# Separate PSUM banks for the last output pieces, an earlier release of the last down bank, and new landing times for the opening, in a one-core attention and SwiGLU kernel

## The chip, the cores and the metric

The kernel runs on one core of a Trainium2 chip. Times are device microseconds (us) of that core. The engines are TensorE (PE, whose weight loads are shown as PEld), VectorE (DVE), ScalarE (ACT), GpSimd (POOL) and SyncE (SP), which issues most of the DMAs. The metric is the median time of the kernel's runs.

## The reference

The input x has 2048 tokens of 512 values. It is normalised per token, xn. One branch is sliding-window attention with 32 heads of 16 and a window of 256 keys, followed by a projection with wo. The other is a SwiGLU network of width 1792 whose result goes through another silu and gates the attention's output.

```python
x = A_x
xn = _layernorm(x, axis=-1)
s = _A_ref(xn, A_wqkv, A_wo)                # window attention, then @ wo
g = _silu(_B_ref(xn, B_w_gate, B_w_up, B_w_down))
return x + s * g                             # _B_ref: (silu(x@w_gate) * (x@w_up)) @ w_down
```

Everything is float32. The kernel splits the operands of each large product into a high and a low float32r part and adds three products: high by high, high by low and low by high (`PAIRS`).

## The kernel before

**How PE is used.** A product over 128 rows of weights is cut into two halves of 64 rows, half 0 and half 1 (`half(r)`), which lie in the upper and lower half of the PE array and stream side by side. For each output item half 0 makes its matmuls first, into a PSUM bank; then DVE copies one column of the bank (`handover`, L582 to L584, tile `ho`), and half 1 may add its matmuls to the same bank. So half 1 trails half 0 by about one item. `LAG` keeps it at least seven 512-column matmuls behind while half 0 has work.

**The items.** The 2048 tokens are four chunks of 512. Work units come in an order made by `dense_order`: `Proj` (tile a, queries and keys), `Values` (vp), `GateUp` (g and u), `Down` (d, in four quarters q of the hidden width) and `Wo` (s, the output projection). Each unit has two items. An item of `Moving` units (vp, d, s) holds two pieces of 128 tokens, n = 0 and 1, side by side in one bank: columns 0 to 255 and 256 to 511. `act` gives the stationary operand (tokens), `w` the moving one (weights). Attention (tiles b, mt, c, pv) is woven into the dense items through the list `extra`.

**What sets the order.** A planner runs at build time. It keeps a clock for each PE half and a queue for DVE (V), ACT (S), POOL (G) and the DMA queue of SP (D), with a cost for each operation that `do` is given, a ready time and a slack; `pump` issues what is ready. Nothing of this runs on the chip: the result is one fixed order of instructions on each engine, and on the chip each engine waits for semaphores in that order. A change of a ready time or a cost moves instructions throughout the program.

**The opening.** `load_first` loads the first 512 tokens as four tiles `xt` and three pieces of the value weights `wr`, some over ACT's DMA queue, some over SP's. DVE takes mean and variance (L339 to L344); ACT subtracts the mean (`center`, L347); PE transposes (`x_turn`, L443, tiles xp); ACT and DVE make the high and the low part of the transposed tokens (xh in L465, xl in L462). Meanwhile ACT copies the high part of each weight piece (`high`, wh, L392) and POOL subtracts for the low part (`low`, wl, L396). The first items on PE are vp. `lands`, `lanes`, `stream_at` and the last argument of `split` are the times at which the planner takes the first loads to land. `warm_up` fills PE with matmuls of no use to the result (tile warm).

**The last down quarter.** For q = 3 `done` of `Down` makes three steps: `one` (DVE, L893) adds the sum so far in `gp` (SBUF) to the bank, in place; `two` (ACT, L897) takes tanh of the bank into `dt`; `three` (DVE, L900) reads `dt` and the bank and writes `gp`. The bank is free after `three`.

**The end.** The last unit is `Wo` of chunk 3, column half 1, items s3_1_0 and s3_1_1. For the second item the products of half 0 with k = 2 and 3 are taken out of half 1 and done in a separate group, `rest` (L587, planned by `rest_pairs`), whose two pieces share one bank. When a piece of an item is complete, `last_part` makes `mul` (L1077: half of gp by the bank into `yl`), then `add` (L1083 on DVE for the second item, which adds `yr`; L1085 on POOL for the first) and stores it; `yr` is made from `rest` by L1047 and L1052. The last store is issued by ACT, the others by SP.

Of the kernel before, what the change touches and what calls it, by code (L numbers as in the profile page):

```python
# [60 lines left out]
def tile_window_attention_swiglu_gate(  # L61
# [258 lines left out]
    def load_first():  # L320
# [8 lines left out]
        lands = (3.8, 4.75, 6.4, 7.3)  # L329
# [57 lines left out]
        def split(raw, j, r, t):  # L387
# [18 lines left out]
            for a in (0, 512):  # L406
# [6 lines left out]
                do("S", t, 0.53, lambda a=a: high(a), done, 0.3 + 0.001 * a)  # L413
# [13 lines left out]
        free_at["D"] = 6.8  # L427
        free_at["S"] = 4.7
        stream_at[0] = 5.7
        lanes[:] = [5.4, 6.3, 6.4, 7.2, 7.3, 7.8, 8.2, 9.2]  # L430
        for i in range(4):
            do("V", lands[i], 1.05 if i != 1 else 1.45, lambda i=i: stats(i), lambda t, i=i: after_stats(t, i), -1.0)
        split(wr[0], 0, 0, 5.5)
        split(wr[1], 1, 1, 8.3)
        split(wr[1], 1, 0, 9.3)

    def x_turn(i):
# [10 lines left out]
        if i == 0:  # L448
            warm_up(warm, 1)
# [341 lines left out]
    class Values(Moving):  # L791
# [12 lines left out]
        def mms(self, i, r, pb):  # L804
# [4 lines left out]
            order = [(t, k, 0, b) for t in range(2) for k in ((0, 1), (2, 3)) for b in range(2)]  # L809
# [11 lines left out]
        def gate(self, i, r, m):  # L821
            if self.c:
                return 0.0
            kp, a, b = (m // 4 % 2, 0, m // 2 % 2) if m < 16 else ((m - 16) // 4, 1, 0)
# [32 lines left out]
    class Down(Moving):  # L857
# [19 lines left out]
        def done(self, i, pb, t, free):  # L877
# [14 lines left out]
            def one():  # L892
                nc.vector.tensor_tensor(p2, g, p2, op=ALU.add)  # L893

            def two():
                tiles.append(take(f"dt{c}_{hf}_{i}", (P, 2, 256)))
                nc.scalar.activation(tiles[0], p2, AF.Tanh, scale=0.5)  # L897

            def three():
                nc.vector.scalar_tensor_tensor(g, tiles[0], 1.0, p2, op0=ALU.add, op1=ALU.mult)  # L900
                give(tiles[0])

            def after_one(t):
                do("S", t, 0.5, two, lambda t: do("V", t, 0.61, three, after_three, PRIO - 0.5), PRIO - 0.5, room(1))

            def after_three(t):
                free(t)
# [7 lines left out]
    class Wo(Moving):  # L915
# [15 lines left out]
        def mms(self, i, r, pb):  # L931
            if r == 0 or (self.c, self.hf) != (NCH - 1, 1):
                yield from super().mms(i, r, pb)
                return
            w = [t.rearrange("p (k n) -> p k n", n=256) for t in self.wts(1)]
            nk = KC - 2 * i
            for t in range(2):
                tok = slice((2 * i + t) * P, (2 * i + t + 1) * P)
                for k in range(nk):
                    for a, b in PAIRS:  # L940
                        def go(first, last, t=t, k=k, a=a, b=b, tok=tok):
                            mm(
                                pb[:, t * 256 : t * 256 + 256], self.act(k, a)[half(1), tok],
                                w[b][half(1), k, :], first, last,
                            )
                            if (t, k, a) == (0, nk - 1, 1):
                                last_part(i, 0, pb, now[0] + 0.35)
# [796 lines left out]
```

## Time and profile before

| | |
|---|---|
| median of 3 runs | 853.81 us (853.38 to 854.67) |
| profiled execution | 852.52 us |
| its span, from the first to the last recorded instruction or landing | 850.6 us |
| outside the span | 1.92 us |
| PE busy | 843.2 us, 99% of the span |
| DVE, ACT, POOL busy | 502.7, 489.2, 630.0 us |
| granted clock of PE | 0.999 |

The profiled execution is 1.29 us below the median of the runs. In the rows, a line number is that of the kernel before (the changed kernel's lines are 2 lower between L448 and the class `Wo`, and the same from there to L1600), L587 is the helper `mm` through which all dense matmuls go, so its rows are told apart by their tiles, and a row of the timeline gives start, duration, engine, line, operation, written and read tiles, shapes and, in brackets, the idle time ahead of it with what ended it.

### The profile page before, as it was taken

To read this page: it belongs to the slowest core of one execution; us is meant where nothing else is said; L and a number is where in the kernel's file an instruction comes from. 1 tells how busy PE (TensorE), PEld (TensorE's weight loads), DVE (VectorE), ACT (ScalarE), POOL (GpSimd) and SP (SyncE) were. 2 spreads that over 40 slices of the span, in tenths; PEclk is the share of its full clock that TensorE was granted. 3 is DMA by queue.
4 is the path that set the end of the run, shared out by engine and by line. 5 is a ranking of instruction groups with operands and counts; after the bars stand their busy time and mean duration, and the time that the engine had idled before them with its cause. 6 is when DMAs were issued, how large, how long until landed. Compare 5 with 4: busy or idle time off the path is not lost.

```text
span 850.6 us, 29962 instructions
## 1 busy us (share of the span) xinstructions
PE 843.2 (99%) x11948; PEld 793.0 (93%) x11948; DVE 502.7 (59%) x1676; ACT 489.2 (58%) x969; POOL 630.0 (74%) x908
## 2 busy tenths in 40 slices
PE   8999999999999999999999999999999999999997
PEld 8999999899999999989999999998999999999897
DVE  4266576656756675655656876565655666653335
ACT  7526664546666557564666657655556665655521
POOL 6639675769777687678777997667689777787861
PEclk9999999999999999999999999999999999999999
DMA  8486847665876995666776977665766688735251
GB/s 205 123 200 141 224 121 208 161 158 114 196 161 195 231 225 125 139 174 167 173 179 166 221 176 193 135 169 132 199 162 169 137 197 187 195 103 138 80 152 53
DMA packets 70098, 140.00 MB, mean 165 GB/s; under 512 B 14710, under 2 KB 23670, under 8 KB 69960
## 3 DMA queue, kind: packets, MB, share of 16 engines
q1 hardware_dynamic: 69496, 137.44, 66.4%
q8 instruction: 94, 1.54, 0.8%
q10 hardware_dynamic: 464, 0.66, 0.3%
q14 instruction: 44, 0.36, 0.2%
HBM read 107.87 MB, written 29.62 MB: 162 GB/s over the span
## 4 chain that ended last, share of the span: by engine, by line
PE 98%; DMA 1%; DVE 0%; SPq 0%; issue 0%; DVEq 0%
PE u L587 20%; PE g L587 19%; PE d L587 19%; PE a L587 10%; PE pv L1414 8%; PE c L1377 6%; PE s L587 6%; PE vp L587 5%; PE b L1229 5%; DMA xt<-x 1%; PE xp L607 0%; PE xp L443 0%; DVE yl L1077 0%; PE mt L1263 0%; PE rest L587 0%; DVE st L339 0%
## 5 line engine op out<-in xcount | busy, mean ns | idle before, releaser
L552 POOL TENSOR_TENSOR wl<-wr,wh 128x512 fp32r<-128x512 f32 (+1 forms) x258 | 305.2, 1197 | 85.4 <-ACT wh L548 58.5
L1237 DVE CUSTOM_DVE_ANT_0 jk<-b,maskb 128x384 bf16<-128x384 f32 (+2 forms) x512 | 271.3, 530 | 103.7 <-PE b L1229 63.1
L587 PE MATMUL d<-wh,hh 64*128 64x256 f32 x1792 | 266.8, 279 | 0.0
L1337 ACT ACTIVATE p<-c 128x512 f32<-128x512 f32 (+2 forms) x384 | 198.0, 571 | 93.2 <-PE c L1377 89.6
L587 PEld LDWEIGHTS d<-wh,hh 64*128 64x128 f32 x1792 | 227.9, 185 | 1.2 <-issue 0.6
L587 PE MATMUL d<-wl,hh 64*128 64x256 f32 x896 | 204.6, 278 | 0.0
L587 PE MATMUL g<-xh,wl 64*128 64x512 f32 x448 | 158.7, 395 | 0.0
L587 PE MATMUL u<-xh,wl 64*128 64x512 f32 x448 | 157.6, 393 | 0.0
L587 PE MATMUL g<-xh,wh 64*128 64x512 f32 x448 | 157.5, 392 | 0.0
L587 PE MATMUL u<-xh,wh 64*128 64x512 f32 x448 | 157.3, 393 | 0.0
L587 PE MATMUL g<-xl,wh 64*128 64x512 f32 x448 | 157.1, 392 | 0.0
L587 PE MATMUL u<-xl,wh 64*128 64x512 f32 x448 | 157.1, 393 | 0.0
L548 ACT ACTIVATE wh<-wr 128x512 fp32r<-128x512 f32 (+1 forms) x258 | 142.8, 589 | 11.1 <-DMA wr<-wgu 3.0
L587 PEld LDWEIGHTS d<-wl,hh 64*128 64x128 f32 x896 | 145.1, 185 | 0.3
L1349 POOL TENSOR_SCALAR_AFFINE_SELECT p<-p 128x256 f32<-128x256 f32 x256 | 102.0, 411 | 38.0 <-ACT p L1337 37.2
L1229 PE MATMUL b<-k,q 48*128 48x384 f32 (+2 forms) x512 | 110.6, 328 | 0.0
L742 POOL TENSOR_TENSOR hh<-h,hh 128x512 fp32r<-128x512 f32 x56 | 72.6, 1297 | 50.3 <-ACT hh L738 49.2
L1353 POOL TENSOR_SCALAR_AFFINE_SELECT p<-p 128x256 f32<-128x256 f32 x224 | 91.6, 411 | 20.2 <-ACT p L1337 18.6
L587 PE MATMUL a<-xl,wh 64*128 64x512 f32 x256 | 96.7, 390 | 0.0
L587 PE MATMUL a<-xh,wl 64*128 64x512 f32 x256 | 96.4, 391 | 0.0
L587 PE MATMUL a<-xh,wh 64*128 64x512 f32 x256 | 96.3, 392 | 0.0
L1377 PE MATMUL c<-q,k 49*128 49x128 f32 (+2 forms) x704 | 95.4, 298 | 0.0
(121 smaller groups left out, 2108.4 us busy)
## 6 DMA issues: line engine op xcount, KB each, us to landing
wr<-wgu SPq DMA_DIRECT2D x112, 256.0 KB
k<-qkd SPq DMA_DIRECT2D x48, 192.0 KB
wr<-wqk SPq DMA_DIRECT2D x32, 256.0 KB
qkd<-qkh SPq DMA_DIRECT2D x32, 256.0 KB
qkd<-qkl SPq DMA_DIRECT2D x32, 256.0 KB
q<-qkd SPq DMA_DIRECT2D x64, 128.0 KB
wr<-wdn SPq DMA_DIRECT2D x32, 256.0 KB
od<-ev SPq DMA_DIRECT2D x32, 256.0 KB
```

What stands on the lines that cost most here:

```text
L548: nc.scalar.activation(wtile[j][0][pr, a:b], raw[pr, a:b], AF.Copy)
L552: nc.gpsimd.tensor_tensor(lo[pr, a:b], raw[pr, a:b], f32(hi[pr, a:b]), op=ALU.subtract)
L587: return nc.tensor.matmul(pb, a, b, start=first, stop=last, skip_group_check=True)
L742: nc.gpsimd.tensor_tensor(hl[:, 1, :], self.h, f32(hl[:, 0, :]), op=ALU.subtract)
L1229: nc.tensor.matmul(pb[:, :n], qs[u % 3][r : r + 48, p, qb * P : (qb + 1) * P], ks[u % 3][r : r + 48, p, lo : lo + n], start=True, stop=True,)
L1237: nc.vector.tensor_tensor_reduce(junk[:, :n], pb[:, :n], maskb[:, 3 * P - n :], 1.0, -3.0e38, ALU.add, ALU.max, m[:, col : col + 1],)
L1337: nc.scalar.activation(t[:, h, :], pc[:, :n], AF.Exp, scale=DH ** -0.5)
L1349: nc.gpsimd.affine_select(s, s, [[0, 2], [1, P]], ALU.is_ge, 0.0, base=0, channel_multiplier=-1)
L1353: nc.gpsimd.affine_select(s, s, [[0, 2], [-1, P]], ALU.is_gt, 0.0, base=0, channel_multiplier=1)
L1377: nc.tensor.matmul(pc[:, at0 : at0 + w], ks[u % 3][r : r + 49, p, k0 : k0 + P], qs[u % 3][r : r + 49, p, qb * P : qb * P + w], start=(i == ...
L1414: nc.tensor.matmul(pbs[r][0][32 * j : 32 * j + 32, q0:q1], vt[half(r), (4 * c + kb) % VT, VW * (4 * g + j) : VW * (4 * g + j) + 32], t[hal ...
```

## The change

It has four parts.

1. **Banks of the last items.** For s3_1_0 and s3_1_1 the second piece of 128 tokens gets a bank of its own, `second[i]` (s2_0 and s2_1), from the pool that attention uses; `rest` gets two banks, rest0 and rest1. `last_part` and `rest_pairs` read the banks given. The planner adds a `handover` copy for each second bank.
2. **Last down quarter.** `one` writes its sum into `gp` instead of the bank, and the bank is free after it; `two` and `three` read `gp`. `three` is planned at 0.8 instead of 0.61 and with a slack of 0.0 instead of -1.0.
3. **Opening times.** `lands`, `lanes`, `stream_at`, `free_at["D"]` and the times of `split` get other values, the latter one for each 512-column piece. One `warm_up` matmul behind the first transposes is left out.
4. **Order in the first vp items.** All products of one pair of k for both token pieces come ahead of the next pair of k, instead of one token piece after the other; `gate` follows.

```diff
-        lands = (3.8, 4.75, 6.4, 7.3)
+        lands = (4.4, 5.5, 7.8, 8.7)
...
-        split(wr[1], 1, 0, 9.3)
+        split(wr[1], 1, 0, (11.9, 11.9))
...
-        if i == 0:
-            warm_up(warm, 1)
...
-            order = [(t, k, 0, b) for t in range(2) for k in ((0, 1), (2, 3)) for b in range(2)]
+            order = [(t, k, 0, b) for k in ((0, 1), (2, 3)) for b in range(2) for t in range(2)]
...
             def one():
-                nc.vector.tensor_tensor(p2, g, p2, op=ALU.add)
+                nc.vector.tensor_tensor(g, g, p2, op=ALU.add)
...
-                nc.scalar.activation(tiles[0], p2, AF.Tanh, scale=0.5)
+                nc.scalar.activation(tiles[0], g, AF.Tanh, scale=0.5)
...
-                nc.vector.scalar_tensor_tensor(g, tiles[0], 1.0, p2, op0=ALU.add, op1=ALU.mult)
+                nc.vector.scalar_tensor_tensor(g, tiles[0], 1.0, g, op0=ALU.add, op1=ALU.mult)
...
             def after_one(t):
-                do("S", t, 0.5, two, lambda t: do("V", t, 0.61, three, after_three, PRIO - 0.5), PRIO - 0.5, room(1))
+                free(t)
+                do("S", t, 0.5, two, lambda t: do("V", t, 0.8, three, after_three, 0.0), PRIO, room(1))
...
+                po = (pb, self.second[i])[t][:, :256]
...
+                        mm(po, self.act(k, a)[half(r), tok], w[b][half(r), k, :], r == 0 and n == 0, r == 1 and end)
+                        if r and end and t == 0:
+                            last_part(i, 0, po, now[0] + 0.35)
...
+                self.second[i] = bank(rb_free, f"s2_{i}")[0]
...
-        pb, tag = bank(rb_free, "rest")
+        pbs = [bank(rb_free, f"rest{n}")[0][:, :256] for n in range(2)]
...
-                y, gp[:, 2 * i + n, 256:512], 0.5, pb[:, 256 * n : 256 * n + 256], op0=ALU.mult, op1=ALU.mult
+                y, gp[:, 2 * i + n, 256:512], 0.5, pb, op0=ALU.mult, op1=ALU.mult
...
+            if isinstance(u, Wo) and (u.c, u.hf) == (NCH - 1, 1):
+                do("V", t, 0.1, lambda: handover(u.second[i]), None, -1.0)
```

Two places show how the rows move. The first is the end of PE's program, where half 0 is in `rest` and half 1 passes from the first to the second token piece of s3_1_0. Before, both pieces of each stand in one bank:

```order
L587 MATMUL s3_1_0_17156<-wl120_17023,xh0_79 128x256
L587 MATMUL rest_17264<-wl120_17023,ox0_16958 128x256
L587 MATMUL s3_1_0_17156<-wh120_17022,xl0_80 128x256
L587 MATMUL rest_17264<-wh120_17022,ox1_16959 128x256
L587 MATMUL s3_1_0_17156<-wh120_17022,xh0_79 128x256
L587 MATMUL rest_17264<-wh120_17022,ox0_16958 128x256
```

Now the same place has a bank for each piece (s2_0 is the second piece of s3_1_0):

```order
L585 MATMUL rest0_17261<-wh120_17124,ox1_16971 128x256
L585 MATMUL s3_1_0_17145<-wl120_17125,xh0_79 128x256
L585 MATMUL rest1_17262<-wh120_17124,ox0_16970 128x256
L585 MATMUL s3_1_0_17145<-wh120_17124,xl0_80 128x256
L585 MATMUL rest1_17262<-wl120_17125,ox0_16970 128x256
L585 MATMUL s2_0_17146<-wh120_17124,xh0_79 128x256
```

The matmuls are the same in number; what they write to is not, and `rest` stands a few matmuls further ahead of half 1.

At the same end DVE's last rows before work on the two pieces of the last item together:

```order
L1047 SCALAR_TENSOR_TENSOR yr1_17297<-gp_83,rest_17264 128x256
L1077 SCALAR_TENSOR_TENSOR yl0_1_17301<-gp_83,s3_1_0_17156 128x256
L1052 TENSOR_TENSOR yr1_17297<-yr1_17297,xr3_1_1_17078 128x256
L1077 SCALAR_TENSOR_TENSOR yl1_0_17311<-gp_83,s3_1_1_17210 128x256
L1077 SCALAR_TENSOR_TENSOR yl1_1_17321<-gp_83,s3_1_1_17210 128x256
L1083 TENSOR_TENSOR yl1_0_17311<-yl1_0_17311,yr0_17282 128x256
L1083 TENSOR_TENSOR yl1_1_17321<-yl1_1_17321,yr1_17297 128x256
```

Now the first piece is finished ahead of the second:

```order
L1047 SCALAR_TENSOR_TENSOR yr1_17296<-gp_83,rest1_17262 128x256
L1077 SCALAR_TENSOR_TENSOR yl0_1_17308<-gp_83,s2_0_17146 128x256
L1052 TENSOR_TENSOR yr1_17296<-yr1_17296,xr3_1_1_17058 128x256
L1077 SCALAR_TENSOR_TENSOR yl1_0_17318<-gp_83,s3_1_1_17204 128x256
L1083 TENSOR_TENSOR yl1_0_17318<-yl1_0_17318,yr0_17280 128x256
L1077 SCALAR_TENSOR_TENSOR yl1_1_17328<-gp_83,s2_1_17205 128x256
L1083 TENSOR_TENSOR yl1_1_17328<-yl1_1_17328,yr1_17296 128x256
```

The first piece's add (L1083) has moved between the two products (L1077).

The second place is the opening on PE, from the first vp matmul to the transposes of the fourth token tile. Before:

```order
L587 MATMUL vp0_0_0_183<-wh0_151,xh1_81 128x256 x2
L587 MATMUL vp0_0_0_183<-wl0_152,xh1_81 128x256 x2
L443 MATMUL xp0_2_191<-ident_68,xt0_2_103 128x128 x2
L443 MATMUL xp0_3_192<-ident_68,xt0_2_103 128x128 x2
L587 MATMUL vp0_0_0_183<-wh0_151,xh1_81 128x256 x2
L587 MATMUL vp0_0_0_183<-wl0_152,xh1_81 128x256 x2
L587 MATMUL vp0_0_0_183<-wh0_151,xh1_81 128x256 x2
L443 MATMUL xp0_2_191<-ident_68,xt0_3_106 128x128 x2
L443 MATMUL xp0_3_192<-ident_68,xt0_3_106 128x128 x2
```

Now:

```order
L585 MATMUL vp0_0_0_178<-wh0_157,xh1_81 128x256 x4
L585 MATMUL vp0_0_0_178<-wl0_158,xh1_81 128x256 x4
L585 MATMUL vp0_0_0_178<-wh0_157,xh1_81 128x256 x3
L443 MATMUL xp0_2_201<-ident_68,xt0_2_103 128x128 x2
L443 MATMUL xp0_3_202<-ident_68,xt0_2_103 128x128 x2
L585 MATMUL vp0_0_0_178<-wh0_157,xh1_81 128x256
L585 MATMUL vp0_0_0_178<-wl0_158,xh1_81 128x256 x4
L443 MATMUL xp0_2_201<-ident_68,xt0_3_106 128x128 x2
L443 MATMUL xp0_3_202<-ident_68,xt0_3_106 128x128 x2
```

The transposes of the third token tile (xt0_2) have moved behind eleven vp matmuls instead of four, those of the fourth (xt0_3) behind sixteen instead of ten.

On ACT the same stretch reads before:

```order
L465 ACTIVATE xh1_81<-xp0_0_154 128x2x256
L347 ACTIVATE xt0_2_103<-xt0_2_103,nm0_90 128x512
L465 ACTIVATE xh1_81<-xp0_1_155 128x2x256
L347 ACTIVATE xt0_3_106<-xt0_3_106,nm0_90 128x512
L392 ACTIVATE wh1_211<-wr1_100 64x512 x3
```

and now:

```order
L463 ACTIVATE xh1_81<-xp0_0_151 128x2x256
L463 ACTIVATE xh1_81<-xp0_1_152 128x2x256
L347 ACTIVATE xt0_2_103<-xt0_2_103,nm0_90 128x512
L392 ACTIVATE wh1_197<-wr1_100 64x512
L347 ACTIVATE xt0_3_106<-xt0_3_106,nm0_90 128x512
L392 ACTIVATE wh1_197<-wr1_100 64x512
```

The second xh copy has moved ahead of the centering of the third tile, and a piece of wh1 between the centerings of the third and the fourth.

More of the change, by code (lines that the diff above doesn't have):

```diff
@@ L976, in done @@
             if (c, hf) == (NCH - 1, 1):
-                last_part(i, 1, pb, t)
+                last_part(i, 1, self.second[i][:, :256], t)
                 return
@@ L1035, in rest_ready @@
             return None
-        return latest([rest["t"], wready.get(len(weighted)), bank_time(rb_free)])
+        return latest([rest["t"], wready.get(len(weighted)), bank_time(rb_free, 2)])
     def rest_pairs():
-        pb, tag = bank(rb_free, "rest")
+        pbs = [bank(rb_free, f"rest{n}")[0][:, :256] for n in range(2)]
         w = [t.rearrange("p (k n) -> p k n", n=256) for t in wtile[len(weighted)]]
@@ L1047, in mul @@
                 nc.vector.scalar_tensor_tensor(
-                    yr, gp[:, 2 + n, 256:512], 0.5, pb[:, 256 * n : 256 * n + 256], op0=ALU.mult, op1=ALU.mult
+                    yr, gp[:, 2 + n, 256:512], 0.5, pbs[n], op0=ALU.mult, op1=ALU.mult
                 )
@@ L1060, in go @@
                 mm(
-                    pb[:, t * 256 : t * 256 + 256], x[a][half(0), k - 2, t * P : t * P + P],
-                    w[b][half(0), k, :], m == 0, m == len(jobs) - 1,
+                    pbs[t], x[a][half(0), k - 2, t * P : t * P + P], w[b][half(0), k, :],
+                    m % 6 == 0, m % 6 == 5,
                 )
```

38 lines of the change are left out of this document (17 added, 21 removed).

## The prediction, made before the changed kernel had run

> **What bounds the kernel now.** I read the page first, for who is busy and what the chain that ended last is made of.
>
> ```profile
> PE 843.2 (99%) x11948; PEld 793.0 (93%) x11948; DVE 502.7 (59%) x1676; ACT 489.2 (58%) x969; POOL 630.0 (74%) x908
> PE 98%; DMA 1%; DVE 0%; SPq 0%; issue 0%; DVEq 0%
> ```
>
> PE is busy 843.2 of 850.6 us, and 98% of the chain lies on PE. The change leaves PE's matmuls what they are (one warm-up matmul apart), so it can win only where PE stands still. The list of PE's waits, the second view, says where that is.
>
> ```profile
> PE warm L242 <- DVE warm L237: 1.1, 1, 1.1
> PE xp L443 <- DVE xt L344: 0.8, 1, 0.8
> PE s L587 <- DVE yl L1077: 0.5, 1, 0.5
> PE rest L587 <- DVE yr L1047: 0.5, 1, 0.5
> PE xp L443 <- issue: 0.4, 1, 0.4
> ```
>
> There are five waits. Three are in the opening, and two are between `s`, `rest` and the DVE operations that read their banks. The table by stretches, the third view, has the same in another form: nothing is lost in the middle, and a good microsecond near the end.
>
> ```profile
> 30.00:826.00 796.00, 796.00 (x11362) 747.94 (x11360) 477.31 (x1604) 464.09 (x921) 606.96 (x878) 1.00 0.69 167
> 841.80:846.50 4.70, 3.62 (x36) 3.01 (x32) 2.77 (x9) 0.00 (x0) 1.52 (x2) 1.00 0.23 84
> ```
>
> PE is busy through all 796 us of the first row and for 3.62 of 4.70 us in the second. So the middle has nothing that this change could give back, and two places remain: the end and the opening.
>
> **The end on PE.** The timeline has it row by row; some matmul records of half 1 are missing there.
>
> ```profile
> 842.04 0.28 PE L587 MATMUL rest<-wl,ox 64*128 64x256 f32 x1
> 842.16 0.28 PE L587 MATMUL rest<-wh,ox 64*128 64x256 f32 x1
> 842.44 0.42 DVE L1077 SCALAR_TENSOR_TENSOR yl<-gp,s 128x256 f32<-128x256 f32 x1 [0.31 <-PE s L587]
> 842.91 0.39 PE L587 MATMUL s<-wh,xh 64*128 64x256 f32 x1 [0.48 <-DVE yl L1077]
> 843.14 0.28 PE L587 MATMUL s<-wl,xh 64*128 64x256 f32 x1
> 843.37 0.28 PE L587 MATMUL s<-wh,xh 64*128 64x256 f32 x1
> 843.64 0.42 DVE L1047 SCALAR_TENSOR_TENSOR yr<-gp,rest 128x256 f32<-128x256 f32 x1 [0.79 <-PE rest L587]
> 844.12 0.38 PE L587 MATMUL rest<-wh,ox 64*128 64x256 f32 x1 [0.47 <-DVE yr L1047]
> 844.34 0.28 PE L587 MATMUL s<-wh,xl 64*128 64x256 f32 x1
> 846.10 0.27 PE L587 MATMUL s<-wh,xl 64*128 64x256 f32 x1
> ```
>
> A slot of a 256-column matmul is 0.12 us (842.04 to 842.16). The next matmul of `s`, the first of its second token piece, starts only at 842.91, just after L1077 has read the first piece out of the same bank; its successor comes at 843.14. Then `rest` does the same: its second piece waits for L1047, and the pair that should follow 843.37 starts at 844.12, the next at 844.34. PE's program is in order, so each wait holds both halves. What is lost against slots of 0.12 is 0.63 + 0.11 + 0.63 + 0.10 = 1.47 us. In the new order the second pieces are s2_0 and rest1, banks that neither L1077 nor L1047 reads. Half 1 is the later half there and has the same 36 matmuls for the last two items, so all 1.47 us comes off the time of the last matmul. What is late next is half 1 itself; the only new waits ahead of it are the two added copies of `handover`, of 0.15 us each, which DVE can make a good microsecond before half 1 arrives, because half 0 has ended those pieces by then.
>
> **The end on DVE.** Behind the last matmul stand four DVE operations and the last store.
>
> ```profile
> 846.41 0.75 DVE L1077 SCALAR_TENSOR_TENSOR yl<-gp,s 128x256 f32<-128x256 f32 x2 [0.55 <-PE s L587]
> 847.08 0.75 DVE L1083 TENSOR_TENSOR yl<-yl,yr 128x256 f32<-128x256 f32 x2
> 847.86 0.35 ACTq L100 DMA_DIRECT2D out<-yl  x1
> ```
>
> The first product starts 0.31 us after the last matmul's start, the second add ends at 847.83, and the store is issued then; from 847.83 to the span's end is 2.77 us, which nothing changes. So DVE ends 1.73 us after the last matmul starts. In the new order only one product and one add are left behind it. Their lengths come from these rows:
>
> ```profile
> 840.64 0.69 DVE L994 SCALAR_TENSOR_TENSOR y<-gp,s 128x512 f32<-128x512 f32 x1 [1.47 <-PE s L587]
> 841.37 0.69 DVE L1001 TENSOR_TENSOR y<-y,xr 128x512 f32<-128x512 f32 x1
> 841.98 0.15 DVE L584 COPY ho<-s 80x1 f32<-80x1 f32 x1
> 844.10 0.42 DVE L1052 TENSOR_TENSOR yr<-yr,xr 128x256 f32<-128x256 f32 x1
> 845.12 0.41 DVE L1077 SCALAR_TENSOR_TENSOR yl<-gp,s 128x256 f32<-128x256 f32 x1
> 845.45 0.42 DVE L1052 TENSOR_TENSOR yr<-yr,xr 128x256 f32<-128x256 f32 x1
> ```
>
> An operation that needs its predecessor's result starts 0.46 us after it (843.64 to 844.10), another 0.33 us after it (845.12 to 845.45). By PE alone the end would come at 0.31 + 0.46 + 0.42 = 1.19 us after the last matmul's start. But without PE's waits DVE has less time for what it does between, so its queue has to be added up. The 36 matmuls take 35 x 0.117 = 4.1 us from first start to last, so half 1 begins them at 846.10 - 1.47 - 4.1 = 840.5, and L994 starts 0.1 later. In the new order follow L1001 and two copies (0.73 and 0.24), the first yr (0.61), seven steps of 0.33 and two of 0.46: the last add starts 0.1 + 0.73 + 0.24 + 0.61 + 2.31 + 0.92 = 4.9 us after that beginning, 0.8 after the last matmul's start, and ends at 1.2 to 1.3. Against 1.73 I take a gain of 0.45. The bounds: 0.54 by PE alone, and a loss of 0.4 if each of the nine steps took 0.46 (then 1.68 + 9 x 0.46 + 0.42 = 6.2 us, 2.1 after the last matmul's start). The value is near the upper end because the rows show 0.33 wherever there is no dependence. The end as a whole: 1.47 + 0.45 = 1.92 us.
>
> **The opening.** It runs on ACT, from the transposes to the first vp matmuls and back.
>
> ```profile
> 8.26 0.60 ACT L465 ACTIVATE xh<-xp 128x512 fp32r<-128x512 f32 x1 [0.20 <-PE xp L443]
> 8.86 0.72 ACT L347 ACTIVATE xt<-xt,nm 128x512 f32<-128x512 f32 x1
> 8.91 0.50 PE L587 MATMUL vp<-wh,xh 64*128 64x256 f32 x2
> 9.64 0.66 PE L443 MATMUL xp<-ident,xt 128*128 128x128 f32 x4
> 10.70 1.80 ACT L392 ACTIVATE wh<-wr 64x512 fp32r<-64x512 f32 x3
> 13.48 0.40 PE L587 MATMUL vp<-wh,xh 64*128 64x256 f32 x2
> 5.43 1.90 SPq L100 DMA_DIRECT2D wr<-wv  x3
> ```
>
> Up to the first vp matmul, at 8.91, the same chain holds: the loads of x, L344, the second transposes, the first xh copy. The warm-up matmul that goes lies in a wait of PE. From 8.91 to the second vp item at 13.48 are 4.57 us; 24 vp matmuls of 0.12 and two groups of transposes of 0.66 make 4.20, and 0.37 is left for four changes between the two kinds and waits for ACT. The new order has the same matmuls, transposes and number of changes. ACT's new order meets it: the second xh copy runs from 8.86 to 9.45 and is needed after eight vp matmuls, at 10.0; the third centering ends at 10.2 and is needed at 10.4; one wh1 copy of 0.6 and the fourth centering end at 11.5, needed at 11.8. The wh1 copy needs its load, issued at 5.43, of which this trace shows only that it had landed by 10.70; if it lands then, the fourth centering ends at 12.0 and 0.2 us is lost. So the opening is worth between a loss of 0.2 and a gain of 0.37, and I take 0.1, since the rows leave only the waits in the 0.37 to win. After 13.48 half 0 and half 1 have the same matmuls as before, in pairs that differ by a few; at four slots of 0.12 that is 0.5 us either way, and I put it at nothing.
>
> **The middle.** The new costs reshuffle the whole program, but the planner keeps the rules under which the trace shows no wait of PE between 20 and 840 us; a gain is excluded by the 796.00 above, and a loss is bounded by one wait like the 0.8 us of the list. I take nothing. The steps of the last down quarter stand 16 times in the trace.
>
> ```profile
> L893 DVE TENSOR_TENSOR d<-gp,d 128x512 f32<-128x512 f32 x16 | 11.1, 692 | 3.1 <-PE d L587 2.7
> L900 DVE SCALAR_TENSOR_TENSOR gp<-dt,d x16: 681/686/689, 215.6 to 835.6; 128x512 f32<-128x512 f32 x16
> L279 DVE TENSOR_SCALAR xt<-xt,nm,rs x6: 533/732/1506, 123.0 to 495.8; 128x512 f32<-128x512 f32 x6
> 123.39 1.47 POOL L742 TENSOR_TENSOR hh<-h,hh 128x512 fp32r<-128x512 f32 x1
> ```
>
> `one` keeps its kind, and its 692 ns; the bank comes free earlier, by the length of `two` and `three`, but no row shows PE waiting for it. `three` gets a second operand in SBUF. Its nearest row is L1001, with both operands in SBUF and 0.69 us, while POOL is idle: that is no change from 686 ns. The other end is L279, which works in SBUF alone and took from 533 to 1506 ns, the longest (from 123.63) beside the POOL operation at 123.39. If `three` took 1506 ns each time, it would cost 16 x 0.82 = 13.1 us of DVE, which is idle for 41% of the span and hides it, unless a `handover` stands behind. I take nothing here.
>
> **The sum.** 1.92 + 0.1 + 0 = 2.0 us. The profiled execution took 852.52 and would take 850.5; its span would be 848.6. The median of the runs is 1.29 higher, so the forecast is 853.81 - 2.0 = 851.8 us.
>
> **The rivals.**
>
> *DVE takes the end back.* PE's waits go, but the nine steps of DVE take 0.46 each, and 0.4 of the 1.47 is lost again: 1.07 with nothing from the opening, 852.7 us. For it: DVE had 1.47 us more for the same work before. Against it: the spacing of 0.33 at 845.12. Chance 0.14.
>
> *The banks are not what PE waited for.* Then the waits stay behind the new names, and only the order of DVE's last operations and the opening are won, 0.55: 853.3 us. Against it: each wait ends within 0.1 us of the one operation that reads the bank, and the two copies that stand between are short. Chance 0.06.
>
> *A new wait in the middle.* A load or a copy that the new order puts too late costs about one wait of the list's size, 0.8 to 1.0: 852.7 us. For it: thousands of rows move. Against it: the old order, by the same rules, has none. Chance 0.09.
>
> *GpSimd and DVE stand in each other's way, and it is slower than before.* Each `three` waits for the POOL operation that runs (POOL is busy 74% of the span, with operations of up to 1.47 us), and the `handover` copy behind it on DVE keeps half 1 from its bank. Half 1 follows half 0 by seven slots of 0.23 us, about 1.6 us, so a delay of 0.82 is mostly absorbed; if half of it, 0.41, shows at each of the 16, the cost is 6.6 us and the time 853.81 - 2.0 + 6.6 = 858.4 us. The kernel is slower than before by more than a measurement tells from 0.23 us each (3.7 us in all). Speaking for it: the spread of L279 against the 681 to 689 ns of L900, which reads one operand from PSUM. Against it: one DVE operation with two SBUF operands, L1052 at 845.45, kept its 0.42 us while POOL began an addition. Chance 0.11. The Trainium skill, in "SBUF — State Buffer", section "Who interferes with whom", states it as a rule: a VectorE instruction with two SBUF inputs contends with a GpSimd instruction that reads SBUF, and whoever comes second is blocked for the other's whole length. By that rule the change does the wrong thing to `three`; the trace agrees as far as L279 goes, with its 1506 ns, but no run here yet shows a two-operand operation so delayed.
>
> **How the numbers follow.** Single runs before lie 1.3 us apart, so I count a difference under 0.2% of the median, 1.7 us, as no change. The forecast has the remaining chance, 0.60, with 850.9 to 852.6 as its own range (a full 0.54 on DVE, 0.37 and the four slots in the opening on the one side; half the DVE gain, the opening's 0.2 and two slots lost on the other); it is under 852.1 in 0.53 and over it in 0.07. The rivals between add 0.14 + 0.06 + 0.09, so within 0.2% is 0.36, and slower is 0.11. The range reaches from 850.5 (that best case, and 0.4 us for the scatter of the runs on the low side) to 853.7 (the banks that do not help, and the same scatter); it leaves out the slower case.
>
> **What would show it.** In the changed kernel's trace the two waits for L1077 and L1047 should be missing from the list of PE's waits; the matmuls of `s` should stand 0.12 apart to the last; DVE should end 1.2 to 1.3 us after the last matmul's start. The second vp item should start at about 13.4. L898, the new `three`, should show near 0.69; a spread up to 1.5, or waits of PE for `ho`, would be the slower rival. A DVE end later than 1.7 us after the last matmul would be the first rival. A PE wait between 20 and 840 us would make the sum wrong.

## The result and the profile after

The changed kernel takes 863.50 us (median of five runs, 862.93 to 865.34) against 854.25 for the kernel before (853.38 to 855.38): a ratio of 1.0110, with a 95% interval of 1.0095 to 1.0126. It is slower by some 9 us where the prediction had it 2 us faster.

The page of the changed kernel's profile (span 861.2 us, 10.6 more than before) and its chain by engine:

```profile
PE 848.8 (99%) x11946; PEld 792.6 (92%) x11946; DVE 511.0 (59%) x1678; ACT 488.6 (57%) x969; POOL 632.5 (73%) x908
PE 91%; DMA 4%; DVE 2%; SPq 1%; issue 0%; ACT 0%; DVEq 0%; ACTq 0%
```

PE's share of the chain falls from 98% to 91%. The list of PE's waits says what took its place:

```profile
PE b L1229 <- DVE m L1237: 4.5, 2, 3.3
PE b L1229 <- DMA k<-qkd: 1.4, 1, 1.4
PE warm L242 <- DVE warm L237: 1.1, 1, 1.1
PE mt L1263 <- DVE m L1237: 0.8, 1, 0.8
PE xp L443 <- DVE xt L344: 0.6, 1, 0.6
```

The waits for L1077 and L1047 are gone, as forecast. New are 6.7 us in which PE stands for attention: for the row maxima m (L1237, made by DVE from the bank `b`), whose late reading keeps the bank, and for a load of k. The 4.5 us are two waits, of 3.3 us until 224.1 and of 1.2 us until 461.2. Two stretches of the timeline of DVE show why a maximum was late there:

```profile
218.35 0.69 DVE L891 TENSOR_TENSOR gp<-gp,d 128x512 f32<-128x512 f32 x1
218.95 4.66 DVE L898 SCALAR_TENSOR_TENSOR gp<-dt,gp 128x512 f32<-128x512 f32 x1
223.54 0.55 DVE L1237 CUSTOM_DVE_ANT_0 jk<-b,maskb 128x384 bf16<-128x384 f32 x1
...
457.87 2.77 DVE L898 SCALAR_TENSOR_TENSOR gp<-dt,gp 128x512 f32<-128x512 f32 x1
460.56 0.14 DVE L582 COPY ho<-a 80x1 f32<-80x1 f32 x1
460.63 0.54 DVE L1237 CUSTOM_DVE_ANT_0 jk<-b,maskb 128x384 bf16<-128x384 f32 x1
```

and the timeline of POOL what ran meanwhile at the first of them:

```profile
218.75 0.75 POOL L1349 TENSOR_SCALAR_AFFINE_SELECT p<-p 128x256 f32<-128x256 f32 x2
219.47 0.40 POOL L1353 TENSOR_SCALAR_AFFINE_SELECT p<-p 128x256 f32<-128x256 f32 x1
219.84 1.27 POOL L550 TENSOR_TENSOR wl<-wr,wh 128x512 fp32r<-128x512 f32 x1
221.08 0.40 POOL L1349 TENSOR_SCALAR_AFFINE_SELECT p<-p 128x256 f32<-128x256 f32 x1
221.44 0.40 POOL L1353 TENSOR_SCALAR_AFFINE_SELECT p<-p 128x256 f32<-128x256 f32 x1
221.81 1.25 POOL L1151 TENSOR_TENSOR o<-o,r 128x512 f32<-128x512 f32 x1
226.53 0.41 POOL L1349 TENSOR_SCALAR_AFFINE_SELECT p<-p 128x256 f32<-128x256 f32 x1 [3.46 <-ACT p L1337]
```

L898, the product `three` that now has both operands in SBUF, starts 0.2 us after the first of seven operations that POOL runs back to back, and ends only 0.55 us after the last of them (which ends at 223.06). The answer for that line, minimum, median and maximum in ns, of the changed kernel:

```profile
L898 DVE SCALAR_TENSOR_TENSOR gp<-dt,gp x16: 673/778/4660, 219.0 to 849.0; 128x512 f32<-128x512 f32 x16
```

Before, the 16 lay between 681 and 689 ns. The end of the timeline:

```profile
856.80 0.28 PE L585 MATMUL s<-wh,xl 64*128 64x256 f32 x1
856.92 0.28 PE L585 MATMUL s<-wh,xh 64*128 64x256 f32 x1
857.04 0.28 PE L585 MATMUL s<-wl,xh 64*128 64x256 f32 x1
857.16 0.28 PE L585 MATMUL s<-wh,xl 64*128 64x256 f32 x1
857.22 0.49 DVE L1083 TENSOR_TENSOR yl<-yl,yr 128x256 f32<-128x256 f32 x1
857.63 0.41 DVE L1077 SCALAR_TENSOR_TENSOR yl<-gp,s 128x256 f32<-128x256 f32 x1
858.07 0.43 DVE L1083 TENSOR_TENSOR yl<-yl,yr 128x256 f32<-128x256 f32 x1
```

The last matmuls stand 0.12 us apart, and DVE is done 1.34 us after the last one starts (858.50), against 1.73 before.

### The profile page after: what moved, and what is told of

It reads as the page before. It is cut to its first block, busy times and chain, and to the rows that moved or that the text cites. A ratio compares the mean times of both kernels' runs of the same rounds, so it can differ in the third digit from the quotient of the medians.

```text
span 861.2 us, 29906 instructions
## 1 busy us (share of the span) xinstructions
PE 848.8 (99%) x11946; PEld 792.6 (92%) x11946; DVE 511.0 (59%) x1678; ACT 488.6 (57%) x969; POOL 632.5 (73%) x908
## 4 chain that ended last, share of the span: by engine, by line
PE 91%; DMA 4%; DVE 2%; SPq 1%; issue 0%; ACT 0%; DVEq 0%; ACTq 0%
PE d L585 17%; PE g L585 17%; PE u L585 17%; PE a L585 10%; PE pv L1414 8%; PE c L1377 6%; PE s L585 5%; PE vp L585 5%; PE b L1229 5%; DMA q<-qkd 2%; SPq L100 1%; DMA wr<-wgu 1%; DVE gp L898 1%; DMA k<-qkd 1%; DMA xt<-x 1%; PE xp L605 0%
## 5 line engine op out<-in xcount | busy, mean ns | idle before, releaser
L1237 DVE CUSTOM_DVE_ANT_0 jk<-b,maskb 128x384 bf16<-128x384 f32 (+2 forms) x512 | 271.3, 530 | 107.5 <-PE b L1229 68.9
L585 PEld LDWEIGHTS d<-wh,hh 64*128 64x128 f32 x1792 | 230.9, 186 | 0.5 <-issue 0.2
L585 PE MATMUL d<-wl,hh 64*128 64x256 f32 x896 | 210.8, 280 | 0.0
L546 ACT ACTIVATE wh<-wr 128x512 fp32r<-128x512 f32 (+1 forms) x258 | 142.0, 590 | 38.6 <-DMA wr<-wgu 13.4
L585 PE MATMUL g<-xl,wh 64*128 64x512 f32 x448 | 163.2, 395 | 0.0
L585 PE MATMUL u<-xh,wh 64*128 64x512 f32 x448 | 163.0, 394 | 0.0
L585 PE MATMUL g<-xh,wh 64*128 64x512 f32 x448 | 162.9, 395 | 0.0
L585 PE MATMUL u<-xh,wl 64*128 64x512 f32 x448 | 162.4, 394 | 0.0
L585 PE MATMUL u<-xl,wh 64*128 64x512 f32 x448 | 162.4, 393 | 0.0
L585 PE MATMUL g<-xh,wl 64*128 64x512 f32 x448 | 162.0, 394 | 0.0
L585 PEld LDWEIGHTS d<-wl,hh 64*128 64x128 f32 x896 | 150.7, 186 | 0.6
```

The source lines that it names most:

```text
L546: nc.scalar.activation(wtile[j][0][pr, a:b], raw[pr, a:b], AF.Copy)
L585: return nc.tensor.matmul(pb, a, b, start=first, stop=last, skip_group_check=True)
L1237: nc.vector.tensor_tensor_reduce(junk[:, :n], pb[:, :n], maskb[:, 3 * P - n :], 1.0, -3.0e38, ALU.add, ALU.max, m[:, col : col + 1],)
```

## The experiments

All runs at a glance. The median of the kernel before is that of its runs beside them on the same chip; "us" in the last column is the ratio less one, times 854.

| run | median, us | before, us | ratio, 95% interval | us |
|---|---|---|---|---|
| the change | 863.50 | 854.25 | 1.0110 (1.0095, 1.0126) | +9.4 |
| e1 change, tanh in the bank | 859.42 | 853.00 | 1.0067 (1.0045, 1.0089) | +5.7 |
| e2 before, `three` from SBUF | 855.37 | 853.00 | 1.0024 (1.0013, 1.0035) | +2.0 |
| e3 own banks alone | 851.41 | 853.00 | 0.9975 (0.9964, 0.9985) | -2.1 |
| e4 opening alone | 861.52 | 853.00 | 1.0095 (1.0074, 1.0116) | +8.1 |
| e5 one queue number | 859.57 | 853.78 | 1.0073 (1.0057, 1.0089) | +6.2 |
| e6 opening, old number | 861.02 | 853.78 | 1.0089 (1.0072, 1.0105) | +7.6 |
| e7 Down part alone | 859.61 | 853.78 | 1.0065 (1.0050, 1.0079) | +5.6 |
| e8 banks and opening, old number | 858.51 | 853.78 | 1.0058 (1.0044, 1.0071) | +5.0 |
| e9 latency number | 854.76 | 854.38 | 1.0014 (0.9996, 1.0032) | +1.2 |
| e10 cost 0.62 | 853.51 | 854.38 | 0.9992 (0.9981, 1.0003) | -0.7 |
| e11 Down order, tanh in the bank | 865.14 | 854.38 | 1.0123 (1.0107, 1.0139) | +10.5 |
| e12 one warm-up less | 853.64 | 854.38 | 0.9994 (0.9985, 1.0003) | -0.5 |
| e13 opening, short maxima | 860.28 | 854.13 | 1.0078 (1.0055, 1.0100) | +6.7 |
| e14 before, short maxima | 852.13 | 854.13 | 0.9980 (0.9971, 0.9990) | -1.7 |
| e15 change, one SBUF operand | 857.58 | 854.13 | 1.0047 (1.0028, 1.0065) | +4.0 |
| e16 Down order, one SBUF operand | 861.91 | 854.13 | 1.0094 (1.0074, 1.0115) | +8.0 |
| e17 before, 11% more traffic | 854.61 | 853.89 | 1.0005 (0.9995, 1.0015) | +0.4 |
| e18 cost 0.8 | 858.63 | 853.89 | 1.0054 (1.0042, 1.0066) | +4.6 |

My theory after the result (A): operations of DVE with two SBUF operands stand still while POOL runs, and that is the loss. The rival (B): the new order and its loads.

### The product's operands: e2, e1, e15

e2 changes nothing but where the three steps of the kernel before write and read:

```diff
-                nc.vector.tensor_tensor(p2, g, p2, op=ALU.add)
+                nc.vector.tensor_tensor(g, g, p2, op=ALU.add)
-                nc.scalar.activation(tiles[0], p2, AF.Tanh, scale=0.5)
+                nc.scalar.activation(tiles[0], g, AF.Tanh, scale=0.5)
-                nc.vector.scalar_tensor_tensor(g, tiles[0], 1.0, p2, op0=ALU.add, op1=ALU.mult)
+                nc.vector.scalar_tensor_tensor(g, tiles[0], 1.0, g, op0=ALU.add, op1=ALU.mult)
```

> The kernel before in its own order, except that the last sum of a Down piece is written to SBUF and the tanh and the product read it there, so that the product, L900, has both operands in SBUF. Nothing is moved. Theory A: of its 16 products 10 start while GpSimd runs, and these are stretched to between 1 and 5 us; the time rises by 2 to 7 us, to 856 to 861. Theory B: all 16 near 0.69 us and the time stays at 854.25 within 0.8 us.

Measured: 1.0024, 2.0 us, at A's lower edge. Nine of the products start while POOL runs; eight of them are stretched, to between 0.80 and 3.37 us, four of them over 1 us, so fewer and by less than A had it. The product's line in e2:

```profile
L900 DVE SCALAR_TENSOR_TENSOR gp<-dt,gp x16: 687/745/3373, 215.7 to 838.8; 128x512 f32<-128x512 f32 x16
```

The longest of them in e2's timeline, with the first and the last of the six operations that POOL runs beside it without a pause:

```profile
459.92 3.37 DVE L900 SCALAR_TENSOR_TENSOR gp<-dt,gp 128x512 f32<-128x512 f32 x1
458.74 1.31 POOL L552 TENSOR_TENSOR wl<-wr,wh 128x512 fp32r<-128x512 f32 x1
...
462.33 0.42 POOL L1349 TENSOR_SCALAR_AFFINE_SELECT p<-p 128x256 f32<-128x256 f32 x1
```

The same operation in the timeline of the kernel before, with the rows of POOL around it there:

```profile
458.88 0.68 DVE L900 SCALAR_TENSOR_TENSOR gp<-dt,d 128x512 f32<-128x512 f32 x1
458.77 0.44 POOL L1349 TENSOR_SCALAR_AFFINE_SELECT p<-p 128x256 f32<-128x256 f32 x1
459.14 1.34 POOL L552 TENSOR_TENSOR wl<-wr,wh 128x512 fp32r<-128x512 f32 x1
```

Beside such back-to-back work of POOL the product takes 0.68 us with one SBUF operand and 3.37 with two. All engines have their operations in the same order in both, so the operands are the cause. And PE pays for it: its list of waits in e2 has a new first line, a maximum that stands on DVE behind this product (the wait ends at 464.9):

```profile
PE mt L1263 <- DVE m L1237: 2.0, 1, 2.0
```

A's mechanism is shown, but the stop through a whole run of POOL is not the usual one. At another place of e2, where POOL goes on without a pause for 12 us, the product waited for the running operation alone; then POOL's next two were late, taking 1.22 us together where the kernel before has 0.78 (last row):

```profile
450.62 1.21 DVE L900 SCALAR_TENSOR_TENSOR gp<-dt,gp 128x512 f32<-128x512 f32 x1
449.99 1.29 POOL L552 TENSOR_TENSOR wl<-wr,wh 128x512 fp32r<-128x512 f32 x1
451.24 1.22 POOL L1349 TENSOR_SCALAR_AFFINE_SELECT p<-p 128x256 f32<-128x256 f32 x2
...
450.15 0.78 POOL L1349 TENSOR_SCALAR_AFFINE_SELECT p<-p 128x256 f32<-128x256 f32 x2
```

Of the 17 products that start beside a running operation of POOL in e2 and in the changed kernel, 14 waited for no more than that operation; the three others are those at 459.92 in e2 and at 218.95 and 457.87 in the changed kernel. What decides between the two is not shown.

e1 goes the other way, from the changed kernel in its own order:

```diff
-                nc.scalar.activation(tiles[0], g, AF.Tanh, scale=0.5)
+                nc.scalar.activation(p2, g, AF.Tanh, scale=0.5)
-                nc.vector.scalar_tensor_tensor(g, tiles[0], 1.0, g, op0=ALU.add, op1=ALU.mult)
+                nc.vector.scalar_tensor_tensor(g, p2, 1.0, g, op0=ALU.add, op1=ALU.mult)
```

> The changed kernel in its own order, except that the tanh is written to the PSUM bank and the product L898 reads it there, so that it has one operand in SBUF instead of two. Theory A (an operation of DVE with both operands in SBUF stands still until GpSimd pauses): all 16 of L898 near 0.69 us, the 4.66 and 2.77 us ones too, and of the 12.8 us that PE loses about 7.2 come back: 863.5 - 7.2 = 856.3 us. Theory B (the new order of the program and its loads are what costs; the long L898 lie beside work that covers them): L898 may shrink, the time stays at 863.5 within 1 us. A loss against A would come from the bank, which is now held until L898: up to 1 us.

All 16 are short again, but the bank is held longer than the plan has it, and that shows. The line in e1:

```profile
L898 DVE SCALAR_TENSOR_TENSOR gp<-d,gp x16: 676/686/692, 219.9 to 848.6; 128x512 f32<-128x512 f32 x16
```

and in the list of PE's waits:

```profile
PE s L585 <- DVE gp L898: 0.9, 1, 0.9
```

So the 3.7 us that came back (9.4 less 5.7) may be too few; e1's runs also lie far apart, three near 857.7 us and three from 861 to 863. In e15 the product holds no bank:

```diff
-                nc.vector.scalar_tensor_tensor(g, tiles[0], 1.0, g, op0=ALU.add, op1=ALU.mult)
+                nc.vector.bn_stats(g[:, 0, :6], tiles[0].rearrange("p t n -> p (t n)"))
```

> The changed kernel in its own order, where the last product L898 is replaced by an operation of DVE of the same length (statistics of the 512 columns of the tanh, the product left out) that has one operand in SBUF and holds no bank. If the operands cost what the trace of PE shows at 219 and 458 us (7.2 us): 856.3 us. If only the 4.1 us that the tanh in the bank gave back: 859.4 us.

Measured: 857.58 us, between the two figures expected; 5.4 us of the 9.4 are gone, give or take 2 us by the two intervals. L898 is short in e15:

```profile
L898 DVE BATCH_NORM_STATS2 gp<-dt x16: 679/690/696, 219.6 to 843.6; 128x6 f32<-128x512 f32 x16
```

and of PE's waits for attention only these are left:

```profile
PE mt L1263 <- DVE m L1237: 0.8, 1, 0.8
PE b L1229 <- DMA k<-qkd: 0.4, 1, 0.4
```

In the changed kernel's trace PE's waits for m and k are 6.7 us, here 1.2, which is 5.5 us less. The operation of e15 also writes 6 columns instead of 512; since the product of e1 writes all 512 and is as short (676 to 692 ns), it is the second operand that is read from SBUF, and not what is written, that makes it long. In this order the operands are about half of the loss. The other 4.0 us, and the 2.1 that the banks gain besides, have another cause.

### The parts alone: e3, e4, e7

e3 is the first part of the change's diff, e4 the third and fourth, e7 the second, each on the kernel before.

> The kernel before with the own banks for the last items alone. Both theories: the order up to 840 us stays, the waits of PE for L1077 and L1047 go (1.47 us), DVE ends about 0.45 us sooner after the last matmul: 854.25 - 1.9 = 852.3 us. If the banks were not what PE waited for: 853.8 us.

e3 is faster than both kernels: 0.9975, 2.1 us. PE's order differs from the kernel before's only from matmul 10416 of 10526 on. PE's waits in e3 no longer name L1077 and L1047, and the table by stretches has PE busy to the end (4.50 of 4.50 us, where 3.62 of 4.70 were busy before):

```profile
842.70:847.20 4.50, 4.50 (x66) 4.40 (x62) 3.75 (x10) 0.00 (x0) 0.81 (x2) 1.00 0.39 137
```

> The kernel before with the opening alone (its landing times, the order of the first products of Values, one warm-up matmul less). L900 keeps one operand in PSUM. Theory A: L900 stays at 0.69 us, the time rises only by what the loads cost, 33 to 62 us (weights ahead of q and k: 1.5 us) and near 390 to 407 us (1.7 us): 855 to 858 us. Theory B: most of the loss is here, 860 us or more. By my prediction: 854.1 us.

e4 costs 8.1 us with its product L898 (`three`, one operand in the bank) at its old length:

```profile
L898 DVE SCALAR_TENSOR_TENSOR gp<-dt,d x16: 672/685/689, 216.9 to 842.4; 128x512 f32<-128x512 f32 x16
```

That is B. The opening itself is not where it is lost: the second vp item starts at 13.24 us in e4 and 13.30 in the changed kernel, 13.48 before.

> The kernel before with the change of the last Down quarter alone, with its new costs and slack in the planner, so that the order moves too. The operands alone cost 2.0 us in the old order. In an order of its own the cost depends on how often L898 starts while GpSimd runs in a row: 1 to 7 us, 854 to 860 us, with PE waiting behind the long ones. If the new slack kept L898 clear of PE's path: 853.0.

e7 costs 5.6 us. The parts add up to 8.1 + 5.6 - 2.1 = 11.6 us, and the change costs 9.4; each part draws an order of its own.

### What the new order costs: e5, e6, e8

In e4's chain of waits, weight loads stand ahead of a load of q (start, length):

```profile
34.54 5.61 DMA wr<-wgu
40.17 8.95 DMA wr<-wgu
50.48 8.21 DMA wr<-wgu
...
62.54 7.43 DMA q<-qkd
```

One number of the opening puts them there:

```diff
-        free_at["D"] = 6.8
+        free_at["D"] = 7.4
```

e5 is the kernel before with this line; e6 is e4 without it; e8 is e6 with own banks. Theory C put the loss on these loads, theory D on other places of the order.

> The kernel before with one number of the opening changed: the planner takes SP's queue to be free from 7.4 us instead of 6.8. In the order this puts the eighth weight tile's load, wr7, behind three of the first loads that write q and k to memory, where it was ahead of them. Theory C (what the opening costs is this late load and those that follow): the DMA idle stretch from 25 to 31 us gets longer, PE waits between 35 and 75 us, and the time rises to between 856 and 862 us. Theory D (the late load costs only the 1.5 us seen between 35 and 75 us; the rest of the opening's loss is other places of the new order): 854 to 856 us. If the load's place costs nothing: 853.0.

> The opening alone as in the run before, but with that one number left at 6.8 us, so that wr7 stands ahead of the loads of q and k again. Theory C: the loss of 8.5 us goes, 852.5 to 855 us. Theory D: 1.5 us come back, about 860 us.

> The changed kernel without the change of the last Down quarter and with that one number at 6.8 us: own banks and the rest of the opening. Theory C: own banks' gain of 1.6 us and the opening's own small gain, 851 to 852 us, ahead of both kernels. Theory D: about 858 us.

e5 loses 6.2 us, but not where C had it: PE is busy 45.00 us of 30 to 75 there. e6 puts the load back and loses 7.6 all the same. C falls: the late load is not the cause. e8 stands 2.6 us under e6, about the banks' gain in e3.

### Is any other order slower? e9, e10, e12, e18, e11, e16

From here on, theory D says that another order costs by itself, whatever the changed numbers stand for. The controls change one planner number, or the one warm-up matmul, and no other operation:

```diff
-    LAT = {"V": 0.14, "S": 0.17, "G": 0.12}
+    LAT = {"V": 0.15, "S": 0.17, "G": 0.12}
```

```diff
-                do("S", t, 0.5, two, lambda t: do("V", t, 0.61, three, after_three, PRIO - 0.5), PRIO - 0.5, room(1))
+                do("S", t, 0.5, two, lambda t: do("V", t, 0.62, three, after_three, PRIO - 0.5), PRIO - 0.5, room(1))
```

The first is e9, the second e10, the same with 0.8 is e18, and e12 leaves out `warm_up(warm, 1)`.

> A control without any purpose: the kernel before with one number of the planner changed, the delay it counts behind an operation of DVE, 0.15 us instead of 0.14. What is computed and the form of every operation stay; the order changes from the 58th matmul of PE on (7902 of 10526 matmuls keep their place). Theory D (the order before happens to fit the chip, and any other order that the same planner draws loses some us to many short waits): 857 to 862 us. Theory E (the loss is due to what the changed numbers say): 853.4 within 1 us.

> The same kind of control with a smaller reach: the planner's cost of the last product of a Down piece 0.62 us instead of 0.61. The order changes only from the 8471st matmul on, and 14 of 10526 matmuls stand in another place. Theory D: with so few places moved, at most one wait, 853.4 to 854.5 us. Theory E: 853.4.

> The kernel before without the one warm-up matmul, the smallest step of the opening. The planner's clock is not touched by it, but the bank and what follows may be, and the order of PE differs. By my prediction it lies in a wait of PE: 853.4 us. Theory D: if the order of the rest moves, 856 to 862 us; if only names move, 853.4.

> The kernel before with one planner number changed, the cost of the last product of a Down piece 0.8 us instead of 0.61, as the change has it; no operation differs. PE's order changes from the 2438th matmul on. If a draw of the order alone costs (as the queue number did, 5.8 us): 857 to 862 us. If only the opening's draws do: 854.1 within 1 us.

e10 and e12 keep nearly the whole order and cost nothing. e9 moves more: matched by the tiles and columns that they read and write, the longest sequence of matmuls that it has in common with the kernel before is 9049 of PE's 10526. Its time is the same within its interval, so "any other order" is too much said. e18 has 8090 in common and loses 4.6 us, e5 has 6973 and loses 6.2. In these two no operation differs from the kernel before: a new draw of the order alone costs as much as half of the change's loss and more.

Where it goes, I counted from the starts of PE's matmul rows: gaps of over 0.3 us number 30 before, with 11.8 us in all; 37 with 14.2 in e9; 41 with 17.7 in e18. The spans of these profiled executions are 850.6, 852.9 and 856.6, so the gaps grow by as much as the spans; in the changed kernel there are 38 with 20.2 us, 8.4 of its 10.6. A single execution scatters, though: e12, which costs nothing, has 33 gaps with 14.3 us in a span of 852.3. So e9's gaps say nothing, and e18's stand 3.4 us above e12's. Part of this scatter has a name: in the traces of e1, e3, e5, e7, e12, e13, e15 and e17 PE stops behind the opening for 0.6 to 2.3 us at a time while it waits for nothing that the profile shows ("issue"), 0.9 to 4.9 us in a run; in those of the kernel before and the changed kernel no such stop is over 0.2 us. e12 has the order of the kernel before there, e1 and e15 that of the changed kernel, so the order is not what makes these stops; what does is open.

In e18 the gaps that the profile can name are waits of four different kinds (PE's waits in e18, without those that the kernel before has):

```profile
PE mt L1263 <- ACT wh L548: 0.8, 1, 0.8
PE b L1229 <- DMA k<-qkd: 0.7, 1, 0.7
PE c L1377 <- DVE m L1237: 0.4, 1, 0.4
PE u L587 <- issue: 0.3, 1, 0.3
```

e11 and e16 are e7's order with the tanh in the bank, and with the one-operand operation of e15.

> The order of the run with the Down change alone (859.6 us), but with the tanh in the bank, so that the product has one operand in SBUF. What is left is the new order's own cost. Theory D: the operands' share, 2 to 4 us, goes, and 856 to 858 us remain, above 853.4. Theory E (the operands are all that costs in this part): 853.4 within 1 us.

> The same replacement in the order of the run with the Down change alone (859.6 us). If the operands are all that costs there: 853.8 us within 0.8. If its new order costs too: 855 to 858 us.

e11 missed: it is slower than e7 by 4.9 us. In it PE waits for L900 to free the bank, which is at least a part of that, so it tells nothing of the operands:

```profile
PE d L587 <- DVE gp L900: 0.8, 1, 0.8
PE a L587 <- DVE gp L900: 0.6, 1, 0.6
```

e16 surprises: the operands' stalls are gone, and the time is 1.0094, no better than e7's 1.0065. It has 9175 matmuls in common with the kernel before, more than e9, and costs 8.0 us, so how much of the order is kept does not decide the cost. In e7's trace only one wait of PE, of 0.6 us at 456, stands behind a long product, so there was less to win here than in e15. In e16 another wait shows, in POOL's timeline:

```profile
494.84 1.29 POOL L1001 TENSOR_TENSOR y<-y,xr 128x512 f32<-128x512 f32 x1 [3.93 <-DMA xr<-x]
496.08 1.31 POOL L552 TENSOR_TENSOR wl<-wr,wh 128x512 fp32r<-128x512 f32 x1
```

L1001 holds POOL, in order, for 3.93 us until xr has landed; the weights' low parts queue behind it. In e7 the same wait is 1.8 us long. Behind it, at 504.5, a wait of PE for m of 1.7 us ends that e7 does not have. So a stall taken out at one place can be lost again at a load further on; that this is the cause of e16's time is argued, not shown.

### Maxima or loads? e13, e14, e17

```diff
-                    junk[:, :n], pb[:, :n], maskb[:, 3 * P - n :], 1.0, -3.0e38,
+                    junk[:, :P], pb[:, n - P : n], maskb[:, 2 * P :], 1.0, -3.0e38,
```

This, on e4, is e13, and on the kernel before e14.

> The opening alone (861.5 us), nothing moved, but each of the 512 row maxima on DVE takes 128 of its up to 384 columns (part of the maximum is left out), so that it is about 0.27 us instead of 0.53. Theory F (what the opening's order costs is PE's attention steps waiting for DVE's maxima): the time falls by 4 to 8 us, to 854 to 857. Theory G (it is the landing of loads): 860 to 862 us.

> The same shortening in the kernel before, as what the run above is compared with. In it PE waits for no maximum longer than 0.3 us: both theories 853.0 to 854.2 us.

The maxima fall to 292 ns (median), e14 gains 1.7 us (more than expected), and e13 gains no more against e4: 1.0078 and 1.0095, where theory F had 4 to 8 us. That the opening's loss is the length of DVE's maxima is not borne out.

e17 puts behind the load of nearly every weight tile a copy that nobody reads:

```diff
+            if last and spare and u.width >= 512:
+                move(spare.pop(), u.src[half(r), :512])
```

> The kernel before in its own order, with 120 copies of 128 KB from memory to memory added, one behind nearly every weight tile's load in SP's queue (15 MB beside 137 MB, 11% more). Nothing reads them. Theory G (what the new orders cost is loads that land late because the queues are full where they are issued): the loads of q, k and the row maxima land about 0.7 us later behind each copy, PE's attention steps wait for them, and the time rises by 3 to 10 us, to 857 to 864. If PE has slack against the loads everywhere: 854.1 within 1 us, and theory G needs a crowding that is peculiar to the new orders.

1.0005: the queues took the 11% without a loss. The order before has slack against its loads, and queues that are merely fuller are not the cause. Loads that crowd at some place of a new order are not excluded by this: PE waits 1.4 us for a load of k in the changed kernel and 0.7 in e18. What is left open is which property of the old order keeps PE's gaps few.

## Why the prediction was wrong, point by point

**The end on PE: right.** Both waits are gone, and e3 alone gains 2.1 us (1.3 to 3.1 by its interval), where 1.92 had been forecast for the whole end. That the two lie so close is in part luck: in e3's trace DVE ends 1.63 us after the last matmul's start, so of the 0.45 us forecast there only 0.10 came.

**The end on DVE: nearly right in the changed kernel**, 1.34 us behind the last matmul's start against 1.2 to 1.3 forecast.

**The opening itself: right.** The second vp item starts at 13.30 us, forecast about 13.4. One warm-up matmul less costs nothing (e12).

**The last down quarter: the rival was the mechanism, and its price was differently made.** The step that failed is that DVE "is idle for 41% of the span and hides it", with 16 times 0.82 us, 13.1 us of DVE, as the bound. The bound on the sum held: the 16 products of the changed kernel take 9.4 us more than 16 times 0.69. What failed is that this is hidden. The longest wait had been taken to be one operation of POOL, but L898 waited through seven, 4.66 us, so the larger part of the delay (6.1 of the 9.4 us) stands in two of the 16, at the places where PE waited. The rows that were trusted, L1001 beside an idle POOL and L1052, which had begun 0.22 us before POOL's addition (845.67), say nothing on an operation that comes second. And what PE waited for behind it was not `handover` but the row maximum L1237, whose bank PE needs: PE waited for m, 4.5 us, and its list has no `ho`. The rival had a chance of 0.11 and 6.6 us, from 0.41 at each of the 16; the operands cost 5.4 in this order, mostly at two places, and 2.0 in the old, so that the price was near is luck. The rule of the Trainium skill, "SBUF — State Buffer", section "Who interferes with whom", that the one that comes second is blocked for the other's whole instruction, agrees with most of the products: at 450.62 in e2 the wait was for one operation. At three of 17 places the measured stop is longer than one instruction (4.66, 2.77 and 3.37 us).

**The middle: the other step that failed.** "The planner keeps the rules under which the trace shows no wait" took the old order's freedom from waits for a property of the rules. It is not one that every order of these rules has: e18 and e5, drawn by the same rules with one number changed, lose 4.6 and 6.2 us, six to eight times the bound of one 0.8 us wait, and the opening, which was put at 0.1, loses 8.1 through the order behind it. Why these orders are slower stays open.

**The sum.** By the runs the change is the banks, -2.1, the operands, +5.4, and a remainder of 9.4 + 2.1 - 5.4 = 6.1 us for the new order. e15 measures banks and new order together, +4.0; the 6.1 is a difference, of the size of e5 and e6. The terms hold for this order alone: in e7's order the replacement that gave 5.4 us here gave nothing (e16).

## What to carry to other kernels

The order that such a build-time planner makes is a draw: one changed number cost nothing that could be told in e9 and e10, and 4.6 and 6.2 us in e18 and e5. So the kernel has to be measured again when any number of the planner moves; an edit that keeps the order (e3, e2) shows what it is worth, one that redraws it does not. Before an operand is moved from PSUM to SBUF on DVE, look at what POOL runs at that moment, how long its run without a pause is, and what queues behind the operation on DVE.

## What was not expected of the hardware

A DVE product with two SBUF operands that starts beside a running operation of POOL mostly gets its turn when that operation ends, and then POOL's next one is late (1.22 us for two, against 0.78). But at three of 17 places it did not get its turn between two operations of POOL that were queued without a pause: 4.66 us through seven and 2.77 through two in the changed kernel, 3.37 through six in e2. With one operand in PSUM all 16 products of the kernel before took 0.68 to 0.69 us, ten of them started beside a running operation of POOL. And 15.6 MB of copies added to 137 MB of transfers cost nothing that could be measured (0.9995 to 1.0015).
